# One row of wq by half rows instead of two, through DMAs of five and six partitions, and a short first load

## Chip, cores and metric

The kernel runs on one core of a Trainium2 chip. The metric is device time in microseconds, the median of several executions. A single further execution was recorded by the hardware profiler; its rows are what is read below.

## The reference

One token `x` of 1024 values goes through two branches, and a sigmoid gate mixes them.

```python
g = sigmoid((x * gate_w).sum())
# A: attention of 32 query heads over 4 kv heads, 65536 cached positions of 128 values, float32
q = x @ wq                                   # 1024 -> 32*128
scores = q . k_cache * 128**-0.5 ; p = softmax(scores)
a = (p . v_cache) @ wo                       # 4096 -> 1024
# B: a routed SwiGLU feed-forward of width 3584, scaled by sigmoid(x @ w_r), plus x
b = x + ((silu(x @ w_gate) * (x @ w_up)) @ w_down) * sigmoid(x @ w_r)
out = g * a + (1 - g) * b
```

Nothing is reused: every weight and every cached key and value, some 346 MB of float32, is read once for one token.

## The kernel before

The host lays out everything that is read in one array, `flow`, of 128 partitions by `TOTAL` columns of float32, in the order of its use: for each kv head g the parts `q` (its slice of wq, KB = 8 rows of 1024 columns), `k` and `v` (65536 columns each) and `o` (8192 columns of wo), and then `gate`, `up` and `down`. `BEGIN` holds where a part begins. The kernel takes the array in loads of `LOAD` = 14336 columns, which is 56 KiB a partition and 7 MiB in all, into three buffers of the pool `stream` (tile `st`). The function `at(part, first, n)` returns columns of a part and issues, on the SP queue, all loads up to the one that holds them (L102). The first load is cut in two DMAs, the last but one in two and the last in six (`ENDS`).

For the last kv head, only KF = 6 of the eight rows of wq lie in `flow`. The other two are stored apart in `halves`, each as two half rows, so that NH = 4 half rows of 1024 columns lie on 64 partitions. They are brought into the tile `half` by eight small DMAs (L106), issued from `at` behind every third load. Each takes eight partitions, four apart, of 16 KiB each:

```python
eighths = [slice(32 * q + r, 32 * q + r + 29, 4) for q in range(2) for r in range(4)]
```

`queries(g)` (L165) multiplies the rows with `x`; for the last head it takes the half rows first, against `xh`, and then the rows of `flow`. `score_chunk` (L184) multiplies a chunk of keys, `value_chunk` (L209, L211, L214) exponentiates, transposes and multiplies a chunk of values, `project` (L237) multiplies with wo, `up_proj` (L260) does gate and up, and L291 and L298 multiply with `down`. L303 adds the branches, and L304 stores the 4 KiB result. Two small DMAs on the ACT queue come at the start: `xk` (128 partitions of 128 bytes) and `x_row` (four rows of 1 KiB).

The order of the transfers is that of the program, on one queue (q1 in the profile). A new load is issued when the matmuls that read its buffer's last content are done. The instructions of the five engines are themselves brought in by DMA; these transfers stand in the profile as queues q8 and q14.

Of the kernel before, what the change touches and what calls it, by code (L numbers as in the profile page):

```python
# [13 lines left out]
P = 128  # L14
D = 1024
# [7 lines left out]
NM = CH // 512  # L23
NB = CH // P
KB = D // P
KF = 6
NH = 2 * (KB - KF)
NQ = D // 4
FB = F // P
# [4 lines left out]
LOAD = 14336  # L34
PARTS = [("q", 0, KB * D)]
for _g in range(G):
    PARTS += [("k", _g, NCH * CH), ("v", _g, NCH * CH), ("o", _g, HG * D)]
    if _g < G - 1:
        PARTS.append(("q", _g + 1, (KB if _g < G - 2 else KF) * D))
PARTS += [("gate", 0, KB * F), ("up", 0, KB * F), ("down", 0, FB * D)]  # L40
BEGIN = {}
TOTAL = 0
for _n, _g, _l in PARTS:
    BEGIN[_n, _g] = TOTAL
    TOTAL += _l
NLOAD = TOTAL // LOAD
assert NLOAD * LOAD == TOTAL and BEGIN["gate", 0] % LOAD == 0

PIECES = [(0, 192), (192, NQ)]

ENDS = {0: [KB * D, LOAD], NLOAD - 2: [8 * D, LOAD], NLOAD - 1: [6 * D, 10 * D, 12 * D, 13 * D, 13 * D + 768, LOAD]}


@with_exitstack
def gated_mix_kernel(ctx: ExitStack, tc: tile.TileContext, x, vecs, halves, flow, out):

# [13 lines left out]
    nc = tc.nc  # L72
# [16 lines left out]


    half = const.tile([64, NH, HG * DH], F32, name="half")
    eighths = [slice(32 * q + r, 32 * q + r + 29, 4) for q in range(2) for r in range(4)]
    loads = []

    def at(part, first, n):

        i, a = divmod(BEGIN[part] + first, LOAD)
        while len(loads) <= i:
            t = stream.tile([P, LOAD], F32, name="st", tag="st")
            ends = ENDS.get(len(loads), [LOAD])  # L100
            for c0, c1 in zip([0] + ends, ends):
                nc.sync.dma_start(t[:, c0:c1], flow[len(loads), :, c0:c1])  # L102
            loads.append(t)
            if len(loads) % 3 == 0 and eighths:
                rows = eighths.pop(0)
                nc.sync.dma_start(half[rows], halves[rows])  # L106
        return loads[i][:, a : a + n]

    at(("q", 0), 0, 1)

    ident = const.tile([P, P], F32, name="ident")
# [40 lines left out]
    gate = sig[:, 0:1]  # L152
# [6 lines left out]
    def queries(g):  # L159
        ps = ps_s.tile([P, 512], F32, name="ps_q", tag="s")  # L160
        rows = [(xh[:, i, :], half[:, i, :]) for i in range(NH)] if g == G - 1 else []
        rows += [(xp[:, k, :], at(("q", g), k * D, D)) for k in range(KF if g == G - 1 else KB)]
        for i, (xs, ws) in enumerate(rows):
            for j in range(4):
                nc.tensor.matmul(  # L165
                    ps[32 * j : 32 * j + 32, :NQ], xs, ws[:, j * NQ : (j + 1) * NQ],
                    start=(i == 0), stop=(i == len(rows) - 1),
                )
        q_sb = work.tile([P, NQ], F32, name="q_sb")
        nc.vector.tensor_copy(q_sb, ps[:, :NQ])  # L170
        pt = ps_1.tile([P, P], F32, name="ps_m", tag="m")
        for e in range(2):
            nc.tensor.matmul(pt[:, 4 * e : 4 * e + 4], q_sb[:, e * DH : (e + 1) * DH], sel4, start=True, stop=True)  # L173
        for s in range(4):
            nc.vector.tensor_copy(
                qp[:, g % 2, s, 8 * s : 8 * s + 8].rearrange("p (j e) -> p e j", e=2),
                pt[:, :HG].rearrange("p (e j) -> p e j", e=2),
            )

    def score_chunk(g, c, mx):  # L180
        ps = ps_s.tile([P, 512], F32, name="ps_s", tag="s")
        for s in range(4):
            for j in range(4):
                nc.tensor.matmul(  # L184
                    ps[32 * j : 32 * j + 32, :], qp[:, g % 2, s, :], at(("k", g), c * CH + (4 * s + j) * 512, 512),
                    start=(s == 0), stop=(s == 3),
                )
        t = scores.tile([P, 512], F32, name="s", tag="s")
        nc.scalar.activation(t, ps, AF.Copy)  # L189
        nc.vector.tensor_reduce(mx[:, c : c + 1], t, AX.X, ALU.max)  # L190
        return t
# [151 lines left out]
```

## Time and profile before

| | |
|---|---|
| median of 3 runs | 812.78 us (812.67 to 813.03) |
| the profiled execution's own time | 812.75 us |
| its span, from the first to the last instruction | 810.8 us |
| PE busy with matmuls | 425.4 us, 52% |
| granted TensorE clock, mean | 0.719 |
| read from memory | 346.05 MB, 427 GB/s over the span |

Times within the trace are microseconds from the start of the span. The DMA share is the busy part of the core's sixteen DMA engines: 1.00 is all sixteen, 0.12 is two of them.

The records of single DMA packets (queue, start, duration, size) lie under the DMA rows of the profile. They don't name the engine. But an engine starts its next packet within a few ns of the end of the last, and the order of sizes that each engine must go through is known from the program. So the 7912 packets of q1 can be strung into sixteen chains, one for each engine. What these chains show is given below as a table of its own, since no view prints it.

### The profile page before, as it was taken

To read this page: it belongs to the slowest core of one execution; us is meant where nothing else is said; L and a number is where in the kernel's file an instruction comes from. 1 tells how busy PE (TensorE), PEld (TensorE's weight loads), DVE (VectorE), ACT (ScalarE), POOL (GpSimd) and SP (SyncE) were. 2 spreads that over 40 slices of the span, in tenths; PEclk is the share of its full clock that TensorE was granted. 3 is DMA by queue.
4 is the path that set the end of the run, shared out by engine and by line. 5 is a ranking of instruction groups with operands and counts; after the bars stand their busy time and mean duration, and the time that the engine had idled before them with its cause. 6 is when DMAs were issued, how large, how long until landed. Compare 5 with 4: busy or idle time off the path is not lost.

```text
span 810.8 us, 6799 instructions
## 1 busy us (share of the span) xinstructions
PE 425.4 (52%) x3158; PEld 128.1 (16%) x3158; DVE 64.3 (8%) x151; ACT 45.6 (6%) x101; POOL 0.7 (0%) x6
## 2 busy tenths in 40 slices
PE   2354344456445564455743655545455545575475
PEld 1011111113111111112111111122111111121132
DVE  2000020000000020000010200000000200000000
ACT  0000030000000030000000300000000200000000
POOL 0000000000000000000000000000000000000000
PEclk9677667678766687666776667776767766687677
DMA  9999999999999999999999999999999999999995
GB/s 408 410 454 425 436 432 438 426 438 425 440 427 432 438 431 437 427 440 430 436 429 436 425 445 433 428 438 422 445 433 428 436 434 436 428 431 442 419 430 242
DMA packets 8091, 346.48 MB, mean 427 GB/s; under 512 B 1080, under 2 KB 1216, under 8 KB 1472
## 3 DMA queue, kind: packets, MB, share of 16 engines
q1 hardware_dynamic: 7912, 346.04, 98.7%
q8 instruction: 24, 0.39, 0.2%
q10 hardware_dynamic: 152, 0.02, 0.0%
q14 instruction: 3, 0.02, 0.0%
HBM read 346.05 MB, written 0.00 MB: 427 GB/s over the span
## 4 chain that ended last, share of the span: by engine, by line
DMA 79%; PE 18%; DVE 1%; issue 0%; ACT 0%; SPq 0%; ACTq 0%; DVEq 0%
DMA st<-in_flow 77%; PE acc L214 8%; PE ps_s L184 7%; DMA xk<-in_vecs 2%; PE ps_q L165 1%; PE ps_f L260 1%; PE att L237 1%; DVE pt L211 0%; PE ps_m L229 0%; ACT s L209 0%; PE ps_m L173 0%; SPq L102 0%; DVE o_sb L225 0%; DVE mx L190 0%; ACT s L189 0%
## 5 line engine op out<-in xcount | busy, mean ns | idle before, releaser
L184 PE MATMUL ps_s<-st,qp 128*32 128x512 f32 x1024 | 157.3, 778 | 154.8 <-DMA st<-in_flow 153.5
L214 PE MATMUL acc<-st,pt 128*32 128x512 f32 x1024 | 159.2, 786 | 134.2 <-DMA st<-in_flow 125.0
L184 PEld LDWEIGHTS ps_s<-st,qp 128*32 128x32 f32 x1024 | 38.9, 138 | 268.3 <-issue 160.7
L214 PEld LDWEIGHTS acc<-st,pt 128*32 128x32 f32 x1024 | 37.7, 138 | 247.0 <-issue 128.1
L189 ACT ACTIVATE s<-ps_s 128x512 f32<-128x512 f32 x32 | 19.1, 597 | 569.2 <-PE ps_s L184 569.2
L260 PE MATMUL ps_f<-st,xp 128*32 128x448 f32 x256 | 33.7, 694 | 27.2 <-DMA st<-in_flow 27.2
L190 DVE TENSOR_REDUCE mx<-s 128x1 f32<-128x512 f32 x32 | 21.9, 686 | 294.2 <-ACT s L189 294.2
L211 DVE STREAM_TRANSPOSE pt<-s 128x512 f32<-128x512 f32 x32 | 22.7, 711 | 195.5 <-PE acc L214 191.8
L165 PE MATMUL ps_q<-st,xp 128*32 128x256 f32 x240 | 20.2, 487 | 15.4 <-DMA st<-in_flow 15.4
L237 PE MATMUL att<-st,op 128*32 128x256 f32 x256 | 20.8, 493 | 12.8 <-DMA st<-in_flow 11.8
L209 ACT ACTIVATE s<-s,nb 128x512 f32<-128x512 f32 x32 | 22.6, 708 | 10.7 <-DVE nb L205 10.7
L291 PE MATMUL y<-st,hp 128*32 128x256 f32 x216 | 16.5, 470 | 5.3 <-DMA st<-in_flow 5.0
L260 PEld LDWEIGHTS ps_f<-st,xp 128*32 128x32 f32 x256 | 9.7, 136 | 50.2 <-issue 26.6
L237 PEld LDWEIGHTS att<-st,op 128*32 128x32 f32 x256 | 10.1, 138 | 21.9 <-issue 11.9
L165 PEld LDWEIGHTS ps_q<-st,xp 128*32 128x32 f32 x240 | 9.1, 137 | 25.8 <-DMA st<-in_flow 16.4
L291 PEld LDWEIGHTS y<-st,hp 128*32 128x32 f32 x216 | 7.8, 133 | 13.7 <-DMA st<-in_flow 7.1
L265 ACT ACTIVATE row<-ps_f 128x896 f32<-128x896 f32 x2 | 1.8, 917 | 142.6 <-PE ps_f L260 142.6
L225 DVE COPY o_sb<-acc 128x512 f32<-128x512 f32 x4 | 2.8, 691 | 71.4 <-PE acc L214 71.4
L147 PE MATMUL ps_m<-dsum,ones 128*128 128x2 f32 x2 | 0.6, 364 | 13.8 <-DVE dsum L145 13.8
L170 DVE COPY q_sb<-ps_q 128x256 f32<-128x256 f32 x4 | 1.7, 424 | 58.2 <-PE ps_q L165 58.2
L209 ACT ACTIVATION_READ_ACCUMULATOR s<-s,nb 128x1 f32 x32 | 6.0, 186 | 0.0
L229 PE MATMUL ps_m<-sel,o_sb 128*128 128x8 f32 x32 | 4.2, 259 | 2.5 <-DVE o_sb L225 2.5
(59 smaller groups left out, 47.3 us busy)
## 6 DMA issues: line engine op xcount, KB each, us to landing
st<-in_flow SPq DMA_DIRECT2D x44, 7168.0 KB, 42.3
st<-in_flow SPq DMA_DIRECT2D x3, 3072.0 KB, 30.3
st<-in_flow SPq DMA_DIRECT2D x2, 4096.0 KB, 12.2
st<-in_flow SPq DMA_DIRECT2D x1, 2048.0 KB, 36.8
half<-in_halves SPq DMA_DIRECT2D x8, 128.0 KB
st<-in_flow SPq DMA_DIRECT2D x1, 1024.0 KB, 38.7
st<-in_flow SPq DMA_DIRECT2D x1, 512.0 KB, 39.5
st<-in_flow SPq DMA_DIRECT2D x1, 384.0 KB
```

Of the source, the lines that this page charges most:

```text
L165: nc.tensor.matmul(ps[32 * j : 32 * j + 32, :NQ], xs, ws[:, j * NQ : (j + 1) * NQ], start=(i == 0), stop=(i == len(rows) - 1),)
L184: nc.tensor.matmul(ps[32 * j : 32 * j + 32, :], qp[:, g % 2, s, :], at(("k", g), c * CH + (4 * s + j) * 512, 512), start=(s == 0), stop=(s ...
L189: nc.scalar.activation(t, ps, AF.Copy)
L190: nc.vector.tensor_reduce(mx[:, c : c + 1], t, AX.X, ALU.max)
L209: nc.scalar.activation(t, t, AF.Exp, bias=nb, scale=SCALE, accum_out=sums[:, c : c + 1])
L211: nc.vector.transpose(pt, t)
L214: nc.tensor.matmul(acc[32 * j : 32 * j + 32, :], pt[:, 32 * m : 32 * m + 32], at(("v", g), c * CH + m * 512, 512), start=(c == 0 and m < 4 ...
L225: nc.vector.tensor_copy(o_sb, acc.rearrange("p (s d) -> p s d", s=4))
L229: nc.tensor.matmul(ps[:, HG : 2 * HG], o_sb[:, s, :], sel[:, HG * s : HG * s + HG], start=(s == 0), stop=(s == 3))
L237: nc.tensor.matmul(att[32 * j : 32 * j + 32, :], op[:, h, :], at(("o", g), h * D + j * NQ, NQ), start=(g == 0 and h == 0), stop=(g == G - ...
L260: nc.tensor.matmul(ps[32 * j : 32 * j + 32, e, :n], xp[:, k, :], at((part, 0), k * F + (2 * j + e) * n, n), start=(k == 0), stop=(k == KB ...
L291: nc.tensor.matmul(y[32 * j : 32 * j + 32, :], hp[:, b, :], at(("down", 0), b * D + j * NQ, NQ), start=(b == 0), stop=False,)
```

## The change

`KF` becomes 7: seven rows of the last head's wq lie in `flow`, and only one is stored as half rows (NH = 2, 8 KiB a partition on the same 64 partitions). These come in eleven DMAs, issued behind every second load, each taking every eleventh partition: nine of six partitions, two of five. `flow` is 1024 columns longer, and those lie in front: the first load has 1024 columns (`FIRST`, 4 KiB a partition, 512 KiB in all), and 47 loads of 14336 columns follow. The boundaries of the loads thus shift by 1024 columns against all parts ahead of the last head's wq, and stay where they were for all behind it.

```diff
-KF = 6
+KF = 7
 NH = 2 * (KB - KF)
...
-NLOAD = TOTAL // LOAD
-assert NLOAD * LOAD == TOTAL and BEGIN["gate", 0] % LOAD == 0
+FIRST = TOTAL % LOAD
+NLOAD = TOTAL // LOAD + 1
+assert FIRST and (BEGIN["gate", 0] - FIRST) % LOAD == 0
...
-ENDS = {0: [KB * D, LOAD], NLOAD - 2: [8 * D, LOAD], NLOAD - 1: [6 * D, 10 * D, 12 * D, 13 * D, 13 * D + 768, LOAD]}
+ENDS = {NLOAD - 2: [8 * D, LOAD], NLOAD - 1: [6 * D, 10 * D, 12 * D, 13 * D, 13 * D + 768, LOAD]}
...
-    eighths = [slice(32 * q + r, 32 * q + r + 29, 4) for q in range(2) for r in range(4)]
+    sixths = [slice(r, 64, 11) for r in range(11)]
...
-        i, a = divmod(BEGIN[part] + first, LOAD)
+        i, a = divmod(BEGIN[part] + first - FIRST, LOAD)
+        i, a = (i + 1, a) if i >= 0 else (0, BEGIN[part] + first)
         while len(loads) <= i:
             t = stream.tile([P, LOAD], F32, name="st", tag="st")
-            ends = ENDS.get(len(loads), [LOAD])
-            for c0, c1 in zip([0] + ends, ends):
-                nc.sync.dma_start(t[:, c0:c1], flow[len(loads), :, c0:c1])
+            if not loads:
+                nc.sync.dma_start(t[:, :FIRST], flow0)
+            else:
+                ends = ENDS.get(len(loads), [LOAD])
+                for c0, c1 in zip([0] + ends, ends):
+                    nc.sync.dma_start(t[:, c0:c1], flow[len(loads) - 1, :, c0:c1])
             loads.append(t)
-            if len(loads) % 3 == 0 and eighths:
-                rows = eighths.pop(0)
+            if len(loads) % 2 == 0 and sixths:
+                rows = sixths.pop(0)
                 nc.sync.dma_start(half[rows], halves[rows])
...
-        "flow": flow.reshape(P, NLOAD, LOAD).transpose(1, 0, 2),
+        "flow0": flow[:, :FIRST],
+        "flow": flow[:, FIRST:].reshape(P, NLOAD - 1, LOAD).transpose(1, 0, 2),
```

More of the change, by code (lines that the diff above doesn't have):

```diff
@@ L45, with gated_mix_kernel @@
     TOTAL += _l
-NLOAD = TOTAL // LOAD
-assert NLOAD * LOAD == TOTAL and BEGIN["gate", 0] % LOAD == 0
+FIRST = TOTAL % LOAD
+NLOAD = TOTAL // LOAD + 1
+assert FIRST and (BEGIN["gate", 0] - FIRST) % LOAD == 0
 PIECES = [(0, 192), (192, NQ)]
-ENDS = {0: [KB * D, LOAD], NLOAD - 2: [8 * D, LOAD], NLOAD - 1: [6 * D, 10 * D, 12 * D, 13 * D, 13 * D + 768, LOAD]}
+ENDS = {NLOAD - 2: [8 * D, LOAD], NLOAD - 1: [6 * D, 10 * D, 12 * D, 13 * D, 13 * D + 768, LOAD]}
 @with_exitstack
-def gated_mix_kernel(ctx: ExitStack, tc: tile.TileContext, x, vecs, halves, flow, out):
+def gated_mix_kernel(ctx: ExitStack, tc: tile.TileContext, x, vecs, halves, flow0, flow, out):
     nc = tc.nc
```

## The prediction

> **What bounds the kernel now.** I read the page first: the DMA slices, the queues, the chain.
>
> ```profile
> DMA  9999999999999999999999999999999999999995
> ...
> DMA packets 8091, 346.48 MB, mean 427 GB/s; under 512 B 1080, under 2 KB 1216, under 8 KB 1472
> ...
> q1 hardware_dynamic: 7912, 346.04, 98.7%
> q8 instruction: 24, 0.39, 0.2%
> q10 hardware_dynamic: 152, 0.02, 0.0%
> q14 instruction: 3, 0.02, 0.0%
> ...
> DMA 79%; PE 18%; DVE 1%; issue 0%; ACT 0%; SPq 0%; ACTq 0%; DVEq 0%
> ```
>
> The DMA engines are busy in every slice but the last, and the chain that ended last is mostly transfer. TensorE's share of the chain is work done between landings. So the time is set by transfer, and the question is by how many of the sixteen engines. The windows answer it:
>
> ```profile
> core 0: us, PE busy (x) PEld busy (x) DVE busy (x) ACT busy (x) POOL busy (x), PEclk, DMA share, GB/s
> ...
> 600.00:700.00 100.00, 54.58 (x340) 13.37 (x340) 9.94 (x19) 8.14 (x20) 0.00 (x0) 0.70 1.00 433
> ...
> 803.80:806.80 3.00, 2.26 (x36) 0.64 (x28) 0.00 (x0) 0.00 (x0) 0.00 (x0) 1.00 0.12 48
> 806.90:808.20 1.30, 0.65 (x16) 0.32 (x16) 0.48 (x1) 0.00 (x0) 0.00 (x0) 1.00 0.00 0
> ```
>
> In mid-run all sixteen work at 433 GB/s, 27.06 GB/s each. From 803.8 to 806.8 the share is 0.12: two engines of sixteen still carry data, and all else waits for them. The end of the chain of waits says the same (start, length, what):
>
> ```profile
> 766.95 39.98 DMA st<-in_flow
> 806.93 0.04 issue
> 806.98 0.70 PE y L298 x16
> ```
>
> The timeline of TensorE shows what it does meanwhile, with the idle time before each row in brackets:
>
> ```profile
> 785.16 7.93 PE L291 MATMUL y<-st,hp 128*32 128x256 f32 x112 [0.30 <-DVE hp L279]
> 797.49 6.86 PE L291 MATMUL y<-st,hp 128*32 128x256 f32 x80 [4.40 <-DMA st<-in_flow]
> 804.77 1.07 PE L291 MATMUL y<-st,hp 128*32 128x256 f32 x16 [0.42 <-DMA st<-in_flow]
> ```
>
> The last bytes land at 806.93; 3.9 us later the span of 810.8 us ends. TensorE waits for transfers in between (4.40 us, 0.42 us), so it follows them.
>
> Why are two late? Strung into one chain for each engine, as told above, the packet records of q1 give this (from the records, not a view; 16 KiB fetches are those of q8, 8 KiB those of q14):
>
> ```
> chains  half-row packets  fetches          last load's end, us
> 3       8 of 16 KiB       none             802.71 to 802.76
> 3       8 of 16 KiB       one of 8 KiB     803.27 to 803.65
> 2       8 of 16 KiB       three of 16 KiB  806.88 and 806.93
> 2       none              none             797.76 and 797.97
> 6       none              three of 16 KiB  801.97 to 802.32
> ```
>
> No chain ever runs dry: between packets there are only steps of a few ns, and about 0.9 us where an instruction fetch cuts in. So an engine's end is the sum of its work. A fetch of 16 KiB costs (806.9 - 802.74) / 3 = 1.4 us, and (802.1 - 797.87) / 3 = 1.4 us in the other half. Eight half-row packets cost 802.74 - 797.87 = 4.87 us, 0.61 us each; 16,384 B at 27.06 GB/s is 0.605. The late two have both burdens.
>
> That a DMA of eight rows goes to eight engines, one row each, also follows from the page: it counts 1080 packets under 512 B. The 54 DMAs of the stream leave 16 records of 4 bytes each (864), the eight half-row ones 8 each (64), the store 4, `xk` 128 + 16, `x_row` 4: that is 1080. So n rows, for n = 8 and 4, use n engines. The eight chains with half rows are the same eight throughout, and the four with `x_row` are among them.
>
> **Half rows.** Each chain loses eight packets of 16 KiB or none (-4.87 us). If six rows go to six engines and five to five, the first five engines get 11 packets of 8 KiB, and the sixth nine, at 0.31 us (half of 0.61): +3.41 and +2.79 us. The other ten get none. Rows of 8 and 4 bracket 5 and 6; a spread over six is nearest to both. The other bound, all on one engine, is a rival below. [...]
>
> **The row that moves into the stream.** Every engine carries eight partitions more of 4 KiB: 32,768 B at 27.06 GB/s, +1.21 us on all sixteen.
>
> **Sum for each engine.** First five: -4.87 + 3.41 + 1.21 = -0.25 us. Sixth: -0.87. Seventh and eighth: -4.87 + 1.21 = -3.66. The upper eight: +1.21. What matters is where the late two lie. Among the first eight, the four with `x_row` (they show as steps of +0.043 us at 13 us) have no 16 KiB fetch, so the late two are among the fifth to eighth. The 24 fetches go round three times in one fixed order of eight chains: three of the upper half, the late two, three of the upper half. If the round follows the engines' order, these are eight neighbours across the middle: the seventh and eighth, and six above. I take that. Then the ends become:
>
> - late two: 806.93 - 3.66 = 803.27;
> - six above with fetches: 802.32 + 1.21 = 803.53;
> - first six: at most 803.65 - 0.25 = 803.40;
> - last two: 799.2.
>
> The last end moves from 806.93 to 803.53, -3.40 us.
>
> **What follows the transfers.** All but the first load, the half rows and the seventh row come as before, and half rows and fetches lie mostly ahead of the last loads, so each late landing moves by about the same 3.4 us. TensorE's last work waits at 797.49 for a landing (4.40 us), and its work before is itself released by landings that also move. I leave 3.9 us behind the last byte.
>
> **At no cost.** SP issues eleven half-row DMAs for eight, and each stands ahead of the next load in its queue; TensorE runs fewer half rows and one row more. The view of the tile `half` (duration in ns, least, median and most), then the page's groups and DMA issues (the last column is us to landing):
>
> ```profile
> L165 PE MATMUL ps_q<-half,xh x32: 376/376/400, 456.8 to 459.5; 64*32 64x256 f32 x32
> L106 SPq DMA_DIRECT2D half<-in_halves x8: 647/647/803, 2.8 to 372.7; - x8
> ```
>
> ```profile
> L165 PE MATMUL ps_q<-st,xp 128*32 128x256 f32 x240 | 20.2, 487 | 15.4 <-DMA st<-in_flow 15.4
> ...
> st<-in_flow SPq DMA_DIRECT2D x44, 7168.0 KB, 42.3
> ```
>
> A load lands 42.3 us after its issue and takes 7.34 MB / 433 GB/s = 17.0 us, so some 25 us of work is queued ahead. The fastest chain leads the slowest by up to 9.2 us, which leaves 16 us. Against this stand three more issues of 0.65 us and boundaries shifted by 1024 columns (1.2 us): hidden. Without that cover the three issues would cost 1.9 us. TensorE saves 16 matmuls of 376 ns and adds 8 of 487 ns, -2.1 us at 52% use; no gain at the end.
>
> **The first load.** Two rows of the timeline at the start:
>
> ```profile
> 0.73 2.03 SPq L102 DMA_DIRECT2D st<-in_flow  x4
> ...
> 13.17 0.17 DVE L128 COPY xp<-xk 128x8 f32<-128x8 f32 x1 [10.01 <-DMA xk<-in_vecs]
> ```
>
> Each engine has eight packets of 4 KiB, 1.2 us of work, and SP issues a DMA every 0.5 us (2.03 / 4), so the next load is there in time. A short first load holds a whole buffer, but its four matmul steps free it as soon as `xp` is there. `xk` landed with eight stream packets between its own; between 4 KiB packets it can be earlier, between 56 KiB packets, of 2.1 us each, up to 17 us late. With 34 us of loads queued behind, neither reaches the end. At the start the first packets' records are 0.1 to 0.9 us longer than later ones of the same size, so I bound the start at -0.7 to +0.9 us and take 0: the engines start at the same issue.
>
> Sum against the profiled execution: 812.75 - 3.40 = 809.35; the median stands 0.03 us above it: 809.4 us.
>
> **The rivals.**
>
> *The late two are among the first six engines.* If the order of the fetches is not the engines', they are the fifth and sixth. Then one of them gets 11 packets and moves by -0.25 us: 812.5 us, no change. For it: only the round's pattern gives the numbers. Against it: in that round the late two are neighbours, in the middle of upper ones. Chance 0.10.
>
> *Slower: two engines write into one partition group.* [...] Chance 0.09 for the full price, 0.09 for the half.
>
> *The rows aren't spread.* If six and five rows went to one engine, it would carry 64 packets: 802.76 - 4.87 + 1.21 + 64 x 0.31 = 818.9, 12 us later: 824.8 us. Only 8 and 4 are seen to spread. Chance 0.03.
>
> **How the numbers follow.** The forecast has 0.69: 809.4 us, by itself 808.6 to 810.4 (the start's bounds, and 0.1 to 0.4 us by which the ends were sorted). A measurement of this kernel can tell about 0.2%, 1.6 us: faster is below 811.15, slower above 814.4. Faster: the forecast, and 0.01 of the half price: 0.70. Same: the rest of the half price and the first rival, 0.18. Slower: 0.09 + 0.03 = 0.12. The range of 8 in 10 reaches from 808.6 over 811.7 to the 812.5 of the first rival: 808.6 to 812.6.
>
> **What would show it.** In the trace after: the DMA share falls from near 1.00 to 0 within some 1.5 us, with only two chains ending early, and no window of 3 us with 0.12. Last byte at about 803.5. The count of 4-byte records gives the spread: 11 half-row DMAs with 64 records. The two chains of the seventh and eighth engines have three fetches and no half rows. It is wrong if a window of about two engines is still there at 806 (they got half rows), if 8 KiB packets took about 0.6 us, or if stream packets beside them took longer than 2.12 us (partition groups shared), or if one chain is late by over 10 us.

## The result, and the profile after

The changed kernel takes 815.75 us (median of 6 runs, 815.59 to 816.12) against 812.85 us before (812.67 to 813.94). The ratio is 1.0035, with a 95% interval of 1.0024 to 1.0046: it is slower, by 2.9 us, where 809.4 us were forecast. The profiled execution has a span of 813.8 us, 3.0 us more than before.

The page of the kernel after, in the rows that answer to those of before:

```profile
DMA  9999999999999999999999999999999999999995
...
DMA packets 8091, 346.48 MB, mean 426 GB/s; under 512 B 1080, under 2 KB 1216, under 8 KB 1600
...
q1 hardware_dynamic: 7912, 346.04, 98.7%
q8 instruction: 24, 0.39, 0.2%
...
DMA 79%; PE 18%; DVE 1%; issue 0%; ACT 0%; SPq 0%; ACTq 0%; DVEq 0%
```

The bound is the same. The 1080 small packets again leave 64 records for the half-row DMAs, nine of six rows and two of five. So the rows are spread over six and five engines as forecast. The end of the chain of waits and the windows (after PEclk the DMA share and GB/s) show what isn't:

```profile
769.33 40.41 DMA st<-in_flow
809.74 0.04 issue
809.78 0.70 PE y L304 x16
```

```profile
core 0: us, PE busy (x) PEld busy (x) DVE busy (x) ACT busy (x) POOL busy (x), PEclk, DMA share, GB/s
...
803.80:806.80 3.00, 2.61 (x46) 1.15 (x36) 0.00 (x0) 0.00 (x0) 0.00 (x0) 0.92 0.59 234
806.80:809.70 2.90, 2.00 (x32) 0.57 (x24) 0.00 (x0) 0.00 (x0) 0.00 (x0) 1.00 0.06 25
```

The last byte lands at 809.74, not 803.5. From 806.8 to 809.7 the share is 0.06: one engine of sixteen is late, not two. And of the other fifteen, which should all have ended by 803.5, many work until about 806 and the last until 806.7. So there are two faults: one engine is 3 us later than all others, and nearly all others are some 2 to 3.5 us later than forecast.

A second reading finds where the fifteen lost their time. The same windows of the kernel before and then of the kernel after; the half rows of the kernel after come in until about 366 us:

```profile
20.00:380.00 360.00, 179.50 (x1296) 51.67 (x1296) 28.47 (x61) 21.05 (x48) 0.00 (x0) 0.71 1.00 432
400.00:760.00 360.00, 194.89 (x1366) 55.91 (x1362) 28.81 (x60) 21.56 (x49) 0.00 (x0) 0.71 1.00 433
```

```profile
20.00:380.00 360.00, 186.00 (x1360) 52.29 (x1360) 28.91 (x62) 21.05 (x48) 0.00 (x0) 0.73 1.00 430
400.00:760.00 360.00, 184.86 (x1347) 52.83 (x1351) 28.84 (x60) 21.56 (x49) 0.00 (x0) 0.72 1.00 434
```

The share is 1.00 in all four, so no engine idles; yet while half rows come in, the sixteen move 430 GB/s instead of 432, and afterwards as much as before. The view counts a packet whole where it starts, and sixteen packets of 56 KiB are 2.5 GB/s over 360 us, so this difference alone would be thin. With each packet's bytes shared out over its duration, the records give 433.2 GB/s before and 429.7 after in the first window, 433.4 in both in the second: 0.8% of 360 us, 2.9 us. Packets take longer. In the packet records, 74 stream packets of 56 KiB took over 10 ns more than the usual 2116 before, and 271 after (those beside instruction fetches among them). The slow ones stand in bursts at the half-row DMAs, except the first, which slowed two packets by less than 0.1 us. At the second, sixteen packets that start between 54.3 and 55.1 us are 160 to 260 ns slow. All sixteen are under way at 55.1 us, so there is one on each engine; the half-row packets themselves took their normal 309 ns there.

Strung into chains as before, the sixteen engines of the kernel after end so (from the records; the same for some of the experiments below, of the last two only the last end):

```
last load's end, us      before            after             own partitions   five, own   no half rows
five lowest              802.7 to 803.7    805.0 to 806.4    802.2 to 803.0
eighth                   (among these)     802.4             about 799
sixth, three fetches     806.9             809.75            805.8
seventh, three fetches   806.9             806.7             802.9
upper, three fetches     802.0 to 802.3    805.8 to 806.1    803.2 to 803.6
upper, no fetch          797.8, 798.0      801.1, 801.5      about 799
last of all              806.93            809.75            805.8            803.9       804.6
```

That the late one is the sixth engine can be told in the kernel after: its chain has nine half-row packets and three fetches, which only one engine can have.

### The profile page after: what moved, and what is told of

Read it like the earlier page. It is cut to its first block, busy times and chain, and to the rows that moved or that the text cites. A ratio compares the mean times of both kernels' runs of the same rounds, so it can differ in the third digit from the quotient of the medians.

```text
span 813.8 us, 6778 instructions
## 1 busy us (share of the span) xinstructions
PE 417.9 (51%) x3150; PEld 123.4 (15%) x3150; DVE 64.4 (8%) x151; ACT 45.6 (6%) x101; POOL 0.7 (0%) x6
## 2 busy tenths in 40 slices
DMA packets 8091, 346.48 MB, mean 426 GB/s; under 512 B 1080, under 2 KB 1216, under 8 KB 1600
## 4 chain that ended last, share of the span: by engine, by line
DMA 79%; PE 18%; DVE 1%; issue 0%; ACT 0%; SPq 0%; ACTq 0%; DVEq 0%
DMA st<-in_flow 79%; PE acc L220 8%; PE ps_s L190 7%; PE ps_q L171 1%; PE att L243 1%; PE ps_f L266 1%; PE ps_m L235 0%; DVE pt L217 0%; DVE o_sb L231 0%; ACT s L215 0%; SPq L108 0%; DVE mx L196 0%; PE ps_m L179 0%; ACT s L195 0%; PE ps_m L206 0%
## 5 line engine op out<-in xcount | busy, mean ns | idle before, releaser
L220 PE MATMUL acc<-st,pt 128*32 128x512 f32 x1024 | 155.4, 754 | 141.7 <-DMA st<-in_flow 131.9
L171 PE MATMUL ps_q<-st,xp 128*32 128x256 f32 x248 | 22.3, 502 | 31.6 <-DMA st<-in_flow 31.6
L206 PE MATMUL ps_m<-md,ones 128*128 128x128 f32 x8 | 2.3, 370 | 6.9 <-DVE md L204 6.9
```

What stands on the lines that cost most here:

```text
L171: nc.tensor.matmul(ps[32 * j : 32 * j + 32, :NQ], xs, ws[:, j * NQ : (j + 1) * NQ], start=(i == 0), stop=(i == len(rows) - 1),)
L220: nc.tensor.matmul(acc[32 * j : 32 * j + 32, :], pt[:, 32 * m : 32 * m + 32], at(("v", g), c * CH + m * 512, 512), start=(c == 0 and m < 4 ...
```

## The experiments

Theory A has two parts. The sixth engine, not the eighth, is one of the two that are late by instruction fetches, and it got nine of the new packets. And half rows slow the streams, or don't, by the partitions that they go to. In the kernel before, the rows of a half-row DMA lie four partitions apart, from one of 0 to 3 or of 32 to 35 on; such partitions are called own below, all others foreign. The names, and the owner in an expectation below, rest on the author's assumption that each engine fills fixed partitions in the stream. No run shows that, since no record names a partition; the runs show what each pattern costs. Theory B: the time goes to something else in the change, the short first load, eleven DMAs for eight, or their source rows.

**Which engines fetch instructions.** Thirty tiny DMAs were added to the kernel before, fifteen behind load 8 and fifteen behind load 32:

```diff
+            if len(loads) in (8, 32):
+                i0, c = int(len(loads) == 32), 0
+                for m in range(1, 16):
+                    nc.sync.dma_start(half[64 : 64 + m, i0, c : c + 8 * m], halves[:m, 0, : 8 * m])
+                    c += 8 * m
```

> The kernel before with thirty more tiny DMAs on SP: behind load 8 and again behind load 32, fifteen DMAs of 1, 2, ... 15 rows, of 32 bytes times that number each, into unused partitions. If a DMA of n rows uses the n lowest engines, the sizes that a chain of packets goes through name its engine. Its time is not of interest (up to some us slower, since SP issues thirty more DMAs). Theory A (one of the two late engines lies among the six that get the new half rows): the two chains of the lower half with three 16 KiB instruction fetches are the sixth engine and the seventh or eighth. The prediction's reading: they are the seventh and the eighth. If n rows don't go to n engines for all n, the marker packets number other than 120 in each set.

The page has 480 small packets more than before:

```profile
DMA packets 8571, 346.56 MB, mean 421 GB/s; under 512 B 1560, under 2 KB 1696, under 8 KB 1952
```

The 240 rows make 240 packets of data. That leaves 240 records of 4 bytes. The kernel before has 16 of these for a DMA that shows on sixteen chains and 8 for one on eight, so they count the engines: n rows go to n engines for every n from 1 to 15. Behind load 32 the markers of up to seven rows were already queued, so each engine ran through its own as soon as it was done with that load. From the packet records, the marker with which each begins:

```
first marker (rows)   1        2        3        4        5        6        7
at, us                555.16   555.50   555.13   555.86   555.69   556.88   557.99
so it is engine       first    second   third    fourth   fifth    sixth    seventh
```

The engines that begin with the marker of six and of seven rows are 1.0 to 2.9 us behind the five lower ones. Behind load 8 the issues had drained all engines, at 141 us. Since then three fetches with the duration that marks this pair in the round (0.88 us) had come, so one for one engine and two for the other: at 1.4 us each 1.4 and 2.8 us, against 1.4 and 2.5 us measured from the mean of the five. So the late two are the sixth and the seventh. The time of this run, 825.2 us, says nothing here, since thirty more issues drained the engines.

**Own partitions.** The kernel after, with the same eleven DMAs of six and five rows, but to partitions four apart as in the kernel before (three of them to a second slot of the same partitions; the matmuls take that slot too, which isn't shown):

```diff
-    half = const.tile([64, NH, HG * DH], F32, name="half")
-    sixths = [slice(r, 64, 11) for r in range(11)]
+    half = const.tile([64, 2 * NH, HG * DH], F32, name="half")
+    nc.gpsimd.memset(half, 0.0)
+    sixths = list(range(11))
...
-                rows = sixths.pop(0)
-                nc.sync.dma_start(half[rows], halves[rows])
+                d = sixths.pop(0)
+                m, p, i0 = len(range(d, 64, 11)), 32 * (d // 4 % 2) + d % 4, NH * (d // 8)
+                nc.sync.dma_start(half[p : p + 4 * m - 3 : 4, i0 : i0 + NH], halves[d:64:11])
```

> [...] Theory A (packets to partitions of other engines' groups stall the streams, and the sixth engine is one of the late ones): the stalls go, the late sixth engine keeps only -4.87 + 2.79 + 1.21 = -0.87 us against before: 811.9 us, and the share of slow 56 KiB packets falls to that of the kernel before. Theory B (the eleven DMAs, their source rows or the short first load cost the time): 815.7 us as the kernel after. If both late engines were the seventh and eighth and the stalls alone were wrong: 809.4 us.

It took 811.94 us, ratio 0.9989 (0.9980 to 0.9998). That is theory A's number, 3.8 us below the kernel after, with the same number of DMAs, the same packets, the same source rows and the same first load. The window has its rate back (433.2 GB/s by the records), and at the end one engine is left, the sixth, at 805.8:

```profile
20.00:380.00 360.00, 188.97 (x1360) 52.98 (x1360) 28.90 (x62) 21.05 (x48) 0.00 (x0) 0.74 1.00 434
...
803.70:805.80 2.10, 1.71 (x24) 0.57 (x24) 0.00 (x0) 0.00 (x0) 0.00 (x0) 1.00 0.06 25
```

With the rows four partitions apart as in the kernel before, 54 stream packets are over 10 ns slow, against 271 in the kernel after and 74 before.

**The kernel before, with foreign partitions.** One line, by which its eight DMAs take every eighth partition instead of partitions four apart:

```diff
-    eighths = [slice(32 * q + r, 32 * q + r + 29, 4) for q in range(2) for r in range(4)]
+    eighths = [slice(r, 64, 8) for r in range(8)]
```

> [...] Bytes for each engine, number of DMAs, first load and source array are as before. Theory A: in the kernel after, eleven such DMAs with 8 KiB packets cost the late engine some 3.6 us, 0.33 each; eight with 16 KiB packets should cost 2.6 us (by the DMA) to 5.2 us (by the byte): 815.4 to 818.0 us. Theory B: 812.8 us, no change.

822.27 us, ratio 1.0126 (1.0093 to 1.0160), 9.4 us slower. The sign is theory A's, but the price is nearly twice what its upper end said. The eight upper engines bring no half rows here; yet by the packet records they end 6.1 to 6.5 us later than before. Windows of the kernel before, then of this one:

```profile
40.00:420.00 380.00, 197.97 (x1411) 56.51 (x1406) 30.82 (x65) 22.24 (x50) 0.00 (x0) 0.71 1.00 434
440.00:760.00 320.00, 173.36 (x1222) 50.53 (x1218) 25.84 (x56) 18.57 (x44) 0.00 (x0) 0.71 1.00 433
```

```profile
40.00:420.00 380.00, 190.96 (x1384) 54.71 (x1376) 30.94 (x65) 22.24 (x50) 0.00 (x0) 0.71 1.00 426
440.00:760.00 320.00, 171.19 (x1242) 50.13 (x1242) 25.39 (x53) 18.98 (x44) 0.00 (x0) 0.72 1.00 433
```

**No half rows.** KF = 8; the tile `half`, its DMAs and its matmuls go, and the first load has 2048 columns:

```diff
-KF = 7
+KF = 8
```

> The change taken to its end: all eight rows of the last head's wq lie in the stream (KF = 8), there are no half rows at all, and the first load has 2048 columns. Theory A: the late two lose 4.87 us of half rows and gain two rows, 2.41 us: last byte at 804.5, the six upper engines with fetches at 802.3 + 2.4 = 804.7, so -2.2 us: 810.6 us, with hardly any slow packets. Theory B, where the short first load costs: 813.5 us or more; where the eleven half-row DMAs cost by their number or source: 810.6 us as theory A.

810.34 us, ratio 0.9967 (0.9954 to 0.9980). The eight engines with fetches end at 804.3 to 804.6, the other eight at 800.1 to 800.9: the sum held within about 0.3 us for every engine, and a short first load costs nothing that this can see.

```profile
800.90:804.40 3.50, 3.22 (x52) 1.18 (x44) 0.00 (x0) 0.00 (x0) 0.00 (x0) 0.99 0.50 201
```

The share of 0.50 is those eight engines alone.

**Five engines, own partitions.** Both faults mended: the half-stored row comes in seven DMAs of five rows, four partitions apart, and the sixth and seventh engines get none. The host lays it out for this:

```diff
-            if len(loads) % 2 == 0 and sixths:
-                rows = sixths.pop(0)
-                nc.sync.dma_start(half[rows], halves[rows])
+            if len(loads) % 3 == 0 and fifths:
+                d = fifths.pop(0)
+                p, w = 32 * (d // 4) + d % 4, 4 if d < 6 else 2
+                nc.sync.dma_start(half[p : p + 17 : 4, :w], halves[d:35:7, :w])
```

> [...] Cleared tile and four half rows in the matmuls, as in the run before with own partitions. Theory A: the sixth and seventh end at 806.93 - 3.66 = 803.3, the five lowest at most at 803.65 - 4.87 + 1.21 + 3.97 = 804.0, the six upper ones with fetches at 803.5: -2.9 us against before, 809.9 us. If the sixth engine were not the late one, it would gain nothing against the version with own partitions on six engines: 811.9 us.

809.43 us (809.23 to 809.78), ratio 0.9958 (0.9946 to 0.9971). This beats the kernels before and after. Thirteen engines end together, from 803.0 to 803.9, much as the prediction had it for the change: the share is 0.71 over the last 3 us, then 0.

```profile
800.90:803.90 3.00, 2.01 (x32) 0.58 (x24) 0.00 (x0) 0.00 (x0) 0.00 (x0) 1.00 0.71 281
804.00:805.20 1.20, 0.57 (x16) 0.23 (x16) 0.48 (x1) 0.00 (x0) 0.00 (x0) 1.00 0.00 0
```

**In the upper partitions.** The kernel before with its half rows in partitions 64 to 127 (their values of `x` move along, which isn't shown):

```diff
-    half = const.tile([64, NH, HG * DH], F32, name="half")
+    half_ = const.tile([P, NH, HG * DH], F32, name="half")
+    half = half_[64:]
```

> [...] If a foreign packet makes writer and owner share, each loses 0.61 us a DMA: late engines 806.9 + 4.9: 817.7 us. If only the owner pays: 812.8 us (upper ones at 802.1 + 4.9 = 807.0, as late as the late two before). If one-to-one costs nothing and only crowding of two foreign packets does: 812.8 us with hardly a slow packet.

822.37 us, ratio 1.0114 (1.0099 to 1.0130). None of the three prices was right; all three rest on the assumption about owners, which no run shows. The source is that of the kernel before, so the destination alone costs 9.5 us, 1.2 us a DMA, twice the 0.61 us of the first price. And all pay: by the packet records all sixteen engines end 7.5 us or more later than before, also the eight that bring no half rows. The rate falls as in the run with every eighth partition, to 426 GB/s.

```profile
40.00:420.00 380.00, 186.58 (x1383) 54.05 (x1373) 30.83 (x65) 22.24 (x50) 0.00 (x0) 0.71 1.00 426
440.00:760.00 320.00, 173.26 (x1235) 49.60 (x1235) 25.39 (x53) 18.98 (x44) 0.00 (x0) 0.72 1.00 433
```

**Five engines, foreign partitions.** The kernel after with the sixth engine spared, by thirteen DMAs of five rows (the last of four), every thirteenth partition:

```diff
-    sixths = [slice(r, 64, 11) for r in range(11)]
+    sixths = [slice(r, 64, 13) for r in range(13)]
```

> [...] Theory A, if the two faults add: against the kernel after (815.8) the sixth engine loses its nine packets (-2.8 us), and the seventh becomes the last, which ended 3.0 us earlier in that trace; thirteen DMAs stall the streams by 13/11 x 5/6 of the 3.8 us that eleven cost, 3.7: 813.0 us. If the place of the late engine didn't matter and only stalls did: 815.7 us.

811.87 us, ratio 0.9986 (0.9977 to 0.9995). Sparing the sixth engine saves 3.9 us, not 2.8, since the stalls came out smaller as well. Packets of 56 KiB took 2123.6 ns on average, against 2126.0 in the kernel after and 2118.3 with own partitions. Over 360 such packets an engine, that is 1.9 and 2.8 us of stall. So 2.8 of the 3.8 us that foreign partitions cost the kernel after stand in these packets; where the sixth engine lost the rest stays open.

**Shorter bursts.** The kernel after with 22 DMAs of 4 KiB a row, one behind every load:

```diff
-    sixths = [slice(r, 64, 11) for r in range(11)]
+    sixths = [(slice(r, 64, 11), i) for i in range(NH) for r in range(11)]
...
-            if len(loads) % 2 == 0 and sixths:
-                rows = sixths.pop(0)
-                nc.sync.dma_start(half[rows], halves[rows])
+            if sixths:
+                rows, i0 = sixths.pop(0)
+                nc.sync.dma_start(half[rows, i0], halves[rows, i0])
```

> The kernel after, each half-row DMA cut in two of 4 KiB a row, issued one behind every load instead of one of 8 KiB behind every second: the same bytes on the same engines to the same partitions, in bursts half as long and twice as many. The stalls cost 3.8 us in the kernel after, against own partitions (815.75 - 811.94). If they go by the bytes: 815.8 us. If by the number of DMAs: 819.6 us. If short bursts are absorbed (1 KiB packets showed no stall, 16 KiB ones cost some 1.2 us a DMA, 8 KiB ones 0.35), the cost per DMA falls to a quarter or less when the packet is halved: 811.9 + 22 x 0.09 = 813.9 us or less.

818.05 us (815.25 to 820.52, the widest spread here but for the run with every eighth partition), ratio 1.0061 (1.0045 to 1.0077). Half as long and twice as many is worse, between the prices by the byte and by the DMA. The stalls cost 818.05 - 811.94 = 6.1 us in place of 3.8: 0.28 us a DMA for 4 KiB packets, 0.35 for 8 KiB, 1.2 for 16 KiB. With the spread of this run the first price can be anything from 0.15 to 0.39. Short bursts aren't absorbed.

## Why the prediction was wrong

*What bounds the kernel* held: the sum of work on the latest of sixteen engines. The spread over six and five engines, which had only the rows of 8 and 4 behind it, held (64 records), and so did every price of own work: 0.31 us for 8 KiB, 1.21 for the row in the stream, nothing for issues, TensorE or the first load. From the last byte to the end it took 4.1 us, where 3.9 were left. `xp` was there at 4.75 us instead of 13.17, and nobody gained by it:

```profile
4.75 0.17 DVE L134 COPY xp<-xk 128x8 f32<-128x8 f32 x1 [1.65 <-DMA xk<-in_vecs]
```

With these prices the run without half rows came out 0.3 us below its sum, the one with five engines 0.5 us below, and the one with own partitions on it.

*The first step that failed* is "If the round follows the engines' order, these are eight neighbours across the middle: the seventh and eighth". The chains had only shown that the late two lie among the fifth to eighth. The markers show the sixth and the seventh. Among the eight lower chains only the late two have 16 KiB fetches, so the eighth has none, and the eight of the round aren't neighbours. The sixth engine kept its fetches and got nine packets: -0.87 us and not -3.66. In the prediction's own sum the last end becomes 806.93 - 0.87 = 806.06 and not 803.53, 2.5 us later, which makes 811.9 us; the run with own partitions took 811.94. This case is half of the first rival, which had put both among the first six at 0.10.

*The second* is the cost of half rows in foreign partitions, which the sum put at nothing. Its sign is that of the slower rival, with its two chances of 0.09, and one of the prediction's signs of being wrong came with it, stream packets of more than 2.12 us beside the half rows: sixteen at the second DMA of the kernel after, 160 to 260 ns over the usual 2116. The full and the half price of that rival, and the 811.7 us in the range, stand on which engine fills which partitions in the stream, and no run shows that. In its place the runs showed 815.75 - 811.94 = 3.8 us for every eleventh partition against partitions four apart, and that all sixteen streams slow down: one packet on each engine at that second DMA, and the eight engines without half rows by 6.1 us or more at their end in the run with every eighth partition. The packets of `x_row` couldn't have told: these are four of 1 KiB, at 0.046 us each, and no stall at 1 KiB says nothing of 8 KiB; packets of 4 KiB did stall the streams, for 6.1 us in all.

Together the steps close the account: 809.4 + 2.5 + 3.8 = 815.7 us. The 2.5 follows from the prediction's own prices once the engine is known; the 3.8 is only measured. The forecast took one cause for each rival and didn't price two at once.

## What to carry to other kernels

Here all DMA engines were busy nearly to the end (a share of 1.00 from 400 to 760 us), and the time was that of the engine with the most work, at 809.74 us in the kernel after: string the packets into one chain for each engine, add up, and count the instruction fetches too, 1.4 us each here. Where a small DMA writes can cost more than what it brings: 512 KiB of half rows, four partitions apart as in the kernel before, came out on their sum (811.94 us), and in every eleventh partition cost 3.8 us more, which is more than the 3.4 us that the balance was to bring. So time such a DMA with its rows in two patterns. Where an argument needs an engine's number, mark it: tiny DMAs of 1 to 15 rows named the seven lowest engines in one run.

## What the runs showed of the hardware

Half rows in foreign partitions (every eighth or eleventh, or four apart in the upper 64) slowed not only the engines that bring them but all sixteen: 0.28, 0.35 and 1.2 us a DMA for packets of 4, 8 and 16 KiB, by the time of the whole kernel. In the kernel after, the stream packets slowed at one such DMA start within 0.8 us of each other at the second and 1.2 at the third, where each engine has one; at the later ones there are 18 to 30, within 3 to 5 us. The first two prices come from six engines at a time, the last from eight, so size and number of engines aren't told apart. Why engines that bring no half rows stall as well stays open; no run here separates it. Nor does any run tell why four partitions apart cost nothing in the lower 64 (811.94 us, on the sum) and 9.5 us in the upper.

Instruction fetches of 16 KiB fall on eight of the sixteen engines in a fixed round, three each in this kernel. Each takes some 1.4 us from its engine's stream, though a half-row packet of as many bytes took 0.61 in the kernel before. Two of the eight are the sixth and seventh engine.
